# Block sums of w_out on VectorE, fifteen units of a batch's products in its own stretch, M's third quarter in other banks, a reordered end

## The chip, the core and the metric

The kernel runs on one core of a Trainium2 chip, in bf16 products with fp32 accumulation. The metric is the device time of one execution in microseconds (us). The profile calls the engines PE (TensorE), DVE (VectorE), ACT (ScalarE), POOL (GpSimd) and SP (SyncE); PEld is TensorE's weight load.

## The reference

A small two-way attention between x and a state, and then a two-layer network on both results. Every batch b has 8 heads, 512 rows of x, 32 rows of state, 64 columns:

```python
scores = scale * x @ state.T;  a  = softmax(scores);   xread = a @ state    # (8, 8, 512, 64)
scores2 = scale * state @ x.T; a2 = softmax(scores2);  sread = a2 @ x       # (8, 8, 32, 64)
y = concatenate([xread, sread], axis=2).transpose(0, 2, 1, 3).reshape(4352, 512)
h = y @ w_in                  # (4352, 2048)
g = maximum(0.01 * h, h)
out = g @ w_out               # (4352, 512), float32
```

## The kernel before

All work is in an order written out by hand, one in-order queue for each engine. A batch has a stretch of 16 steps. For batch b the kernel folds state and w_in into one matrix M (four quarters of 512 columns, `a_m` with `m_evict`), so that a step of the first layer, `ff1(a, hT, s)`, is two products of 512 columns into a PSUM bank with the tag "ph" (two banks), followed by the relu on ScalarE, which writes block s of hT. Around these products the stretch of batch b prepares the attention of batch b + 1:

- `a_scores` (PSUM tag "sc") needs `a.xT`, which `a_xt_dma` makes with a transposing DMA on SP's queue out of `a.xb`. GpSimd casts `xb` from the loaded `xl` (`cast_x`).
- `a_shift` (row maxima and subtraction), `a_max2`, `a_probs` and `a_probs2` run on VectorE; the exponentials `a_exp` and `a_exp2` on ScalarE.
- `a_a2t` transposes a2 with a DMA into `a2T`, and `a_sread` multiplies it with x (PSUM tag "big").
- `a_m` for quarter 3 of the batch itself comes in step 1, for quarters 0, 1 and 2 of the next one in steps 10, 10 and 13, in the banks "big" and "sc".

The second layer is computed in two ways. Batches 0 and 1 use `piece`: four products of 512 columns, four pieces to a block of 128 rows, and `y_store` copies the finished bank (tag "py") into a tile `ysb` (tag "ysb", three buffers) and issues its store. Batches 2 to 7 and the rows of the state (the last stretch, `hs`) use seven products in place of eight (Winograd's form of Strassen's method): `Batch` and `Fast`. The sums of blocks of hT are VectorE instructions (`Fast.sums`); the four sums of blocks of w_out, `tw`, are made once on GpSimd (`weights_sums`, in two halves). A batch has 56 units `(n, m)`, product n of block pair m, each two products of 256 columns; they run in the order of `Batch.units` in two "py" banks. When a product is complete, `done` copies the bank (`save`, ScalarE) or adds it to a copy (`join`, VectorE), and the results go from `yo0` and `yo1` to DRAM.

The loop hands units out by step: two, or three and four in turn, first those left from the batch before, then those of the batch itself:

```python
            k = OWN if b == 2 else 0
            n = 3 + s % 2 if b > 2 else 2
            left = len(before.units) if before else 0
            if left:
                before.run(min(n, left))
            if n > left:
                now.run(min(n - left, OWN - own))
                own += min(n - left, OWN - own)
```

After the loop, 16 steps of `ff1_s` (the first layer for the state's rows) alternate with units left from batch 7, and then the seven products for the state's rows with the rest.

Of the kernel before, what the change touches and what calls it, by code (L numbers as in the profile page):

```python
# [9 lines left out]
P = 128  # L10
B, H, S, D = 8, 8, 512, 64
NS = 32
# [15 lines left out]
def kernel(  # L28
# [374 lines left out]

    def weights_sums(m0, m1):
        ms = slice(m0, m1)
        for dst, u, v, op in (
            (0, B12, B11, ALU.subtract), (2, B22, B12, ALU.add),
            (1, B11, tw[2], ALU.subtract), (3, tw[1], B21, ALU.add),
        ):
            nc.gpsimd.tensor_tensor(  # L410
                out=tw[dst][:, ms], in0=u[:, ms], in1=v[:, ms], op=op
            )

    class Fast:
# [21 lines left out]

        def unit(self, bank, n, m, first):
# [7 lines left out]
            for i in range(self.sub):  # L445
                nc.tensor.matmul(  # L446
                    bank[:, i, :], lhsT=lhs[:, m, P * i:P * (i + 1)], rhs=rhs[:, m, :],
                    start=(first and m == 0 and i == 0), stop=(m == NM - 1),
                    skip_group_check=True,
                )  # L450
# [13 lines left out]
    class Batch:  # L464
        def __init__(self, b, hT):
            saved = {n: (spool, t, 1) for n, t in ((1, "sv1"), (6, "sv6"), (5, "sv1"), (7, "sv7"))}
            self.b, self.f = b, Fast(hT, 2 * P, [(spool, f"su{n}", 1) for n in range(4)], saved)
            self.units = [(n, m) for n in (1, 2, 6, 5, 7, 3, 4) for m in range(NM)]
            own = [(1, m) for m in range(6)] + [(2, m) for m in range(OWN - 6)]
            self.units = own + [u for u in self.units if u not in own]  # L470
            self.bank = {}
            self.yos = {}
# [5 lines left out]

        def out(self, r):
            nc.sync.dma_start(  # L480
                out[self.b * SROW:self.b * SROW + S, :].rearrange(
                    "(p r i) f -> p r i f", r=2, i=2)[:, r], self.yo(r)[:]
            )

# [38 lines left out]

    OWN = 10

# [251 lines left out]
    for s in range(16):  # L777
# [31 lines left out]

    before = None  # L810
    for b in range(2, B):
        hT = hpool.tile([P, 16, S], BF16, name="hT", tag="hT")
# [4 lines left out]
        if b == 2:  # L817
            std = [(i, 3) for i in range(2)] + [(i, jq) for i in range(2, NT) for jq in range(4)]
        own = 0
        for s in range(16):  # L820
            ff1(a, hT, s)
            if s == 0:
# [7 lines left out]
            elif s == 1:  # L830
# [5 lines left out]
                if b + 2 < B:  # L836
                    cast_x(b + 2, 0, 8, POO)
                if b == 2:
                    weights_sums(4, 8)
            elif s == 3:  # L840
                if before:
                    before.f.sums(2)
                if nxt is not None:
                    a_max2(nxt)
            elif s == 4:
                if b == 2:
                    load_state(1)
            elif s == 6:
                if b == 2:
                    a_sread(a1)  # L850
                if before:
                    before.f.sums(3)
            elif s == 8:
                a_sread(a)
                if b == 2:
                    state_t(1)
            if s == 11:
                for n in (0, 1):
                    now.f.sums(n, 0, 4)
            if nxt is not None:  # L860
                if s == 5:
                    a_exp(nxt)
                elif s in (6, 7):
                    a_exp2(nxt, s - 6)
                    if s == 7:
                        a_probs(nxt)
                        a_probs2(nxt)
                elif s == 10:
                    pm0 = a_m(nxt, 0, "big")
                    pm1 = a_m(nxt, 1, "sc")  # L870
                    m_evict(nxt, 0, pm0, VEC)
                    m_evict(nxt, 1, pm1, SCA)
                elif s == 13:
                    m_evict(nxt, 2, a_m(nxt, 2, "big"), SCA)
                if s == 13 and b + 2 < B:
                    a_open(att_of[b + 2], b + 2)
                    a_xt_dma(att_of[b + 2])
            if std:
                i, jq = std.pop(0)
                piece(1, h1, i, jq)  # L880
                continue
            k = OWN if b == 2 else 0
            n = 3 + s % 2 if b > 2 else 2
            left = len(before.units) if before else 0
            if left:
                before.run(min(n, left))
            if n > left:
                now.run(min(n - left, OWN - own))
                own += min(n - left, OWN - own)
        before = now  # L890
# [9 lines left out]
    for j in range(16):  # L900
        ff1_s(hs, j)
        before.run(1 + j % 2)
        if j == 5:
            before.f.sums(2)
        elif j == 8:
            before.f.sums(3)
        elif j in (9, 11):
            fs.sums((j - 9) // 2, 0, 4)
    for n in (0, 1):
        fs.sums(n, 4, 8)  # L910
    u = psum.tile([P, 1, HC], FP32, name="yu", tag="big", bufs=1)[:]
    v = psum.tile([P, 1, HC], FP32, name="yv", tag="sc", bufs=1)[:]
    ysb = [ypool.tile([P, 1, DM], FP32, name="yhs", tag="ysb") for _ in range(2)]

    def out_s(i):
        for bb in range(4):
            r0 = (4 * i + bb) * SROW + S
            nc.sync.dma_start(out[r0:r0 + NS, :], ysb[i][NS * bb:NS * (bb + 1), 0, :])

    for n in (1, 2, 6, 5, 7, 3, 4):  # L920
        bank = v if n in (2, 5, 3) else u
        for m in range(NM):
            fs.unit(bank, n, m, first=n in (1, 2, 5, 4))
        if n in (1, 6, 5, 7):
            fs.save(n, bank)
        if n == 1:
            fs.sums(2)
        elif n == 2:
            fs.join(ysb[0][:, :, :HC], bank, 1)
            fs.sums(3)  # L930
        elif n == 7:
# [6 lines left out]
        elif n == 4:  # L938
            fs.join(ysb[1][:, :, :HC], bank, 7)
            out_s(1)  # L940
        if n != 4:
            before.run(min(4, len(before.units)))
    before.run(len(before.units))

# [29 lines left out]
```

## Time and profile before

| | us |
|---|---|
| median of 3 runs | 223.9 (223.79 to 224.22) |
| the profiled execution | 223.65 |
| its span, first to last instruction | 221.9 |
| TensorE busy | 202.4 |
| VectorE busy | 151.0 |
| ScalarE busy | 142.2 |
| GpSimd busy | 48.9 |

The span is what the trace shows; the profiled execution's own time lies 1.75 us above it. TensorE's products are pipelined, so its busy time is not a count of useful cycles; gaps between the starts of its instructions say more.

### The profile page before, as it was taken

The numbers are of one execution on the slowest core, as the hardware profiler recorded it, in microseconds if no ns is written. First come the engines' busy times: TensorE is split into PE (matmuls) and PEld (weight loads), VectorE is DVE, ScalarE is ACT, GpSimd is POOL, SyncE is SP. The second block draws the span as 40 slices with busy tenths as digits, with TensorE's granted clock in tenths as the row PEclk, the third lists the DMA queues.
The fourth block names the chain that finished last, engine by engine and source line by source line (L and its number), as shares of the span: only waits on it lengthen the run. The fifth ranks groups of instructions, "written<-read, shape, count | busy, mean of one in ns | idle before, by whom it ended". The sixth has DMA issues, their size and how long they took to land.

```text
span 221.9 us, 4381 instructions
## 1 busy us (share of the span) xinstructions
PE 202.4 (91%) x1804; PEld 127.3 (57%) x1804; DVE 151.0 (68%) x205; ACT 142.2 (64%) x266; POOL 48.9 (22%) x53
## 2 busy tenths in 40 slices
PE   7999999856999778999999999999999999999980
PEld 2543434322345335666666666665666677788870
DVE  1778597089978958997799689967995613360340
ACT  3468575809869736796679677966796766556210
POOL 8830002098009910320015003200020002000210
PEclk9999999999999969999999999999999999999996
DMA  6999994991187059104990595058003300300025
GB/s 205 210 207 294 203 258 92 262 244 33 27 230 219 3 126 251 26 3 133 246 144 4 144 266 112 3 124 211 1 3 145 92 3 35 154 3 0 3 109 175
DMA packets 38020, 27.74 MB, mean 125 GB/s; under 512 B 24304, under 2 KB 34672, under 8 KB 38000
## 3 DMA queue, kind: packets, MB, share of 16 engines
q1 hardware_dynamic: 33072, 21.04, 38.2%
q0 software_dynamic: 4784, 6.29, 14.0%
q8 instruction: 14, 0.23, 0.4%
q10 hardware_dynamic: 144, 0.13, 0.2%
q14 instruction: 6, 0.05, 0.1%
HBM read 17.30 MB, written 8.91 MB: 118 GB/s over the span
## 4 chain that ended last, share of the span: by engine, by line
PE 44%; DVE 25%; DMA 17%; POOL 5%; issue 5%; SPq 1%; POOLq 0%; DVEq 0%
PE yq L446 19%; PE ph L347 8%; DMA xT<-xb 7%; DMA w_in_bf<-in_moe_w_in_dram 5%; PE pyw L375 3%; PE ph L358 3%; DMA out_dram<-ysb 3%; DVE mrowb L223 3%; DVE mrow L215 3%; DMA xl<-in_x_dram 3%; DVE su L435 3%; PE py L375 2%; DVE M L340 2%; POOL tw_xf L410 2%; DVE aT L247 2%
## 5 line engine op out<-in xcount | busy, mean ns | idle before, releaser
L352 ACT ACTIVATE hT<-ph 128x512 bf16<-128x512 f32 x112 | 66.3, 600 | 33.2 <-PE ph L347 32.5
L347 PE MATMUL ph<-aT,M 128*128 128x512 bf16 x224 | 66.2, 381 | 2.6 <-ACT hT L352 2.6
L446 PEld LDWEIGHTS <-su 128*128 128x128 bf16 x416 | 40.0, 98 | 16.5 <-issue 4.8
L446 PEld LDWEIGHTS <-hT 128*128 128x128 bf16 x288 | 27.6, 99 | 13.4 <-issue 4.2
L446 PE MATMUL yq<-tw_xf,su 128*128 128x256 bf16 x192 | 27.6, 272 | 2.0 <-DVE yo L458 2.0
L347 PEld LDWEIGHTS <-M 128*128 128x128 bf16 x224 | 21.8, 98 | 11.9 <-issue 4.4
L446 PE MATMUL yq<-w_out_bf,hT 128*128 128x256 bf16 x192 | 27.3, 278 | 0.0
L375 PE MATMUL py<-w_out_bf,hT 128*128 128x512 bf16 x96 | 24.2, 379 | 2.3 <-DVE ysb L384 2.3
L435 DVE TENSOR_TENSOR su<-hT 128x1024 bf16<-128x1024 bf16 (+1 forms) x18 | 16.6, 924 | 12.1 <-ACT hT L352 12.1
L514 POOL TENSOR_TENSOR yo<-sv,sv 128x512 f32<-128x512 f32 x6 | 8.0, 1330 | 75.7 <-ACT sv L455 53.1
L105 POOL CAST xb<-xl 128x2048 bf16<-128x2048 f32 (+1 forms) x6 | 10.7, 1776 | 63.2 <-DMA xl<-in_x_dram 63.2
L458 DVE TENSOR_TENSOR yo<-yq,sv 128x512 f32<-128x512 f32 x18 | 12.3, 686 | 16.6 <-PE yq L446 16.6
L375 PEld LDWEIGHTS <-hT 128*128 128x128 bf16 x128 | 11.9, 98 | 16.8 <-issue 3.7
L340 ACT CAST M<-pm 128x1024 bf16<-128x1024 f32 x18 | 18.2, 1011 | 5.0 <-PE pm L326 4.9
L455 ACT COPY sv<-yq 128x512 f32<-128x512 f32 x24 | 14.0, 585 | 3.3 <-PE yq L446 3.2
L446 PE MATMUL yq<-tw_x,hT 128*128 128x256 bf16 x96 | 13.5, 273 | 0.0
L446 PE MATMUL yq<-w_out_bf,su 128*128 128x256 bf16 x96 | 13.5, 273 | 0.0
L446 PE MATMUL yq<-tw_x,su 128*128 128x256 bf16 x96 | 13.4, 273 | 0.0
L340 DVE CAST M<-pm 128x1024 bf16<-128x1024 f32 x9 | 11.0, 1218 | 1.7 <-PE pm L326 1.7
L215 DVE TRANSPOSE_TENSOR_REDUCE mrow<-sc 128x32 f32<-128x1024 f32 x7 | 8.7, 1248 | 4.5 <-PE sc L205 4.5
L273 ACT ACTIVATE e<-sc,mcols 128x512 bf16<-128x512 f32 x16 | 11.1, 700 | 0.4 <-DVE mcols L267 0.4
L326 PE MATMUL pm<-w_in_bf,st_t 64*32 64x512 bf16 x192 | 8.9, 391 | 2.7 <-DVE M L340 2.7
(124 smaller groups left out, 270.1 us busy)
## 6 DMA issues: line engine op xcount, KB each, us to landing
out_dram<-yo SPq DMA_DIRECT2D x12, 512.0 KB, 2.9
xl<-in_x_dram SPq DMA_DIRECT2D x5, 1024.0 KB, 6.6
w_in_bf<-in_moe_w_in_dram POOLq DMA_DIRECT2D x4, 512.0 KB, 9.3
w_out_bf<-in_moe_w_out_dram POOLq DMA_DIRECT2D x4, 512.0 KB, 16.7
out_dram<-ysb SPq DMA_DIRECT2D x8, 256.0 KB, 5.1
xf<-in_x_dram SPq DMA_DIRECT2D x2, 512.0 KB, 5.1
x<-in_x_dram POOLq DMA_DIRECT2D x2, 512.0 KB, 13.7
xl<-in_x_dram POOLq DMA_DIRECT2D x1, 1024.0 KB, 18.5
```

Of the source, the lines that this page charges most:

```text
L105: copy(xs[b][:, :, h0:h1].rearrange("p t h d -> p h t d"), xl[b][:, h0:h1].rearrange("p h (t d) -> p h t d", t=NT),)
L215: nc.vector.tensor_reduce(out=m1[:], in_=flat.rearrange("p (c j) -> p c j", j=NS), axis=AX.X, op=ALU.max, apply_transpose=True,)
L273: nc.scalar.activation(out=a.e2[:, g], in_=a.sc[:, g, :], func=AF.Exp, bias=a.m2s[:, g:g + 1], scale=SCALE, accum_out=a.r2[:, g:g + 1],)
L326: nc.tensor.matmul(at[v][NS * r:NS * (r + 1)], lhsT=st_of(a, g, k), rhs=w_in_bf[D * g:D * (g + 1), k, DM * c:DM * (c + 1)], start=True, st ...
L340: copy(a.M[:, :, cols], pm[:])
L347: nc.tensor.matmul(ph[:], lhsT=a.M[:, g, P * j:P * (j + 1)], rhs=a.aT[:, g, :], start=(g == 0), stop=(g == 1),)
L352: nc.scalar.activation(out=hT[:, j, :], in_=ph[:], func=AF.Prelu, alpha=0.01)
L375: nc.tensor.matmul(y.py, lhsT=hT[:, j, P * i:P * (i + 1)], rhs=w_out_bf[:, j, :], start=(j == 0), stop=(j == 15),)
L435: (eng or nc.vector).tensor_tensor(out=S[n][:, ms], in0=u[:, ms], in1=v[:, ms], op=op)
L446: nc.tensor.matmul(bank[:, i, :], lhsT=lhs[:, m, P * i:P * (i + 1)], rhs=rhs[:, m, :], start=(first and m == 0 and i == 0), stop=(m == NM ...
L455: copy(t[:], bank)
L458: nc.vector.tensor_tensor(out=dst, in0=bank, in1=self.sv[n][:], op=ALU.add)
```

## The change

- `y_store` gives batch 0's blocks 2 and 3 the tags `yo0` and `yo1` (one buffer each), which the batches from 2 on use for their results. The other six blocks share the three buffers of "ysb".
- The sums of w_out's blocks become four VectorE instructions over all eight pairs, two in step 3 and two in step 8 of batch 2. `weights_open` only allocates, and moves ahead of the loop.
- A batch runs 15 of its 56 units in its own stretch in place of 10: six of product 1, six of product 2, and then (1, 6), (2, 6), (1, 7). The number of units per step is in two lists, `PACE` and, for batch 2, `PACE2`. In step 11 the units come ahead of `ff1`.
- The first three quarters of M for the next batch are all multiplied in step 10, behind its units: quarter 0 in "big", 1 in "sc", 2 in the two "ph" banks. VectorE and ScalarE copy one half each of quarter 2; ScalarE then copies quarters 0 and 1.
- `a_xt_dma` for batch b + 2 moves from step 13 to step 11, `a_exp2` from steps 6 and 7 to 7 and 8, `a_probs2` from step 7 to 11, the block sums of hT from step 11 to 12 (three of them), and those for the batch before to steps 2 and 3.
- At the end the units left are spread otherwise, half of the state's stores go to GpSimd's queue, and the last product of batch 7 is computed in two halves of rows, the second in another bank. Each half is joined and stored by itself; the right half of `yo1` is stored ahead of them.

```diff
@@ y_store
-        ysb = ypool.tile([P, DM], FP32, name="ysb", tag="ysb")
+        tag, bufs = (f"yo{i - 2}", 1) if (b, i) in ((0, 2), (0, 3)) else ("ysb", 3)
+        ysb = ypool.tile([P, DM], FP32, name="ysb", tag=tag, bufs=bufs)
@@ the sums of w_out
-    def weights_sums(m0, m1):
-        ms = slice(m0, m1)
-        for dst, u, v, op in (
...
-            nc.gpsimd.tensor_tensor(
-                out=tw[dst][:, ms], in0=u[:, ms], in1=v[:, ms], op=op
-            )
+    def weights_sum(dst):
+        u, v, op = (
+            (B12, B11, ALU.subtract), (B11, tw[2], ALU.subtract),
+            (B22, B12, ALU.add), (tw[1], B21, ALU.add),
+        )[dst]
+        with nc.allow_low_precision(reason="operands of a product"):
+            nc.vector.tensor_tensor(out=tw[dst][:], in0=u[:], in1=v[:], op=op)
@@ Batch
-            own = [(1, m) for m in range(6)] + [(2, m) for m in range(OWN - 6)]
+            own = [(n, m) for n in (1, 2) for m in range(6)] + [(1, 6), (2, 6), (1, 7)]
...
-    OWN = 10
+    OWN = 15
+    PACE = (1, 4, 4, 4, 3, 4, 4, 3, 4, 4, 4, 4, 3, 4, 3, 3)
+    PACE2 = (0,) * 10 + (3, 3, 2, 2, 2, 3)
@@ batch 1's stretch, step 8
             a_sread(a0)
-            weights_open()
-            weights_sums(0, 4)
@@ the loop over batches 2 to 7
+        def fill(s):
+            n = (PACE2 if b == 2 else PACE)[s]
+            left = min(n, len(before.units)) if before else 0
+            if left:
+                before.run(left)
+            if n > left:
+                now.run(n - left)
+
         for s in range(16):
+            if s == 11:
+                fill(s)
             ff1(a, hT, s)
...
                     cast_x(b + 2, 0, 8, POO)
-                if b == 2:
-                    weights_sums(4, 8)
+                if before:
+                    before.f.sums(2, 4, 8)
             elif s == 3:
                 if before:
-                    before.f.sums(2)
+                    before.f.sums(3)
                 if nxt is not None:
                     a_max2(nxt)
+                if b == 2:
+                    weights_sum(0)
+                    weights_sum(2)
...
             elif s == 8:
                 a_sread(a)
                 if b == 2:
                     state_t(1)
-            if s == 11:
-                for n in (0, 1):
+                    weights_sum(1)
+                    weights_sum(3)
+            elif s == 11 and b + 2 < B:
+                a_open(att_of[b + 2], b + 2)
+                a_xt_dma(att_of[b + 2])
+            elif s == 12:
+                for n in range(3):
                     now.f.sums(n, 0, 4)
             if nxt is not None:
                 if s == 5:
                     a_exp(nxt)
-                elif s in (6, 7):
-                    a_exp2(nxt, s - 6)
+                elif s in (7, 8):
+                    a_exp2(nxt, s - 7)
                     if s == 7:
                         a_probs(nxt)
-                        a_probs2(nxt)
-                elif s == 10:
-                    pm0 = a_m(nxt, 0, "big")
-                    pm1 = a_m(nxt, 1, "sc")
-                    m_evict(nxt, 0, pm0, VEC)
-                    m_evict(nxt, 1, pm1, SCA)
-                elif s == 13:
-                    m_evict(nxt, 2, a_m(nxt, 2, "big"), SCA)
-                if s == 13 and b + 2 < B:
-                    a_open(att_of[b + 2], b + 2)
-                    a_xt_dma(att_of[b + 2])
+                elif s == 11:
+                    a_probs2(nxt)
             if std:
                 i, jq = std.pop(0)
                 piece(1, h1, i, jq)
...
+            elif s != 11:
+                fill(s)
+            if s == 10 and nxt is not None:
+                pm0 = a_m(nxt, 0, "big")
+                pm1 = a_m(nxt, 1, "sc")
+                pm2 = a_m(nxt, 2, "ph")
+                for g, copy in enumerate((VEC, SCA)):
+                    copy(nxt.M[:, g, 2 * DM:3 * DM], pm2[g][:])
+                m_evict(nxt, 0, pm0, SCA)
+                m_evict(nxt, 1, pm1, SCA)
@@ the end
-        before.run(1 + j % 2)
+        before.run(1)
...
-            nc.sync.dma_start(out[r0:r0 + NS, :], ysb[i][NS * bb:NS * (bb + 1), 0, :])
+            (nc.gpsimd, nc.sync)[i].dma_start(out[r0:r0 + NS, :], ysb[i][NS * bb:NS * (bb + 1), 0, :])
...
-    for n in (1, 2, 6, 5, 7, 3, 4):
+    before.run(2)
+    for n, more in ((1, 2), (2, 2), (6, 1), (5, 1), (7, 1), (3, 0), (4, 0)):
...
-    before.run(len(before.units))
+        before.run(more)
+    before.run(8)
+    before.out(1, slice(HC, DM))
+    for i in range(2):
+        bank = before.bank[7] if i == 0 else psum.tile([P, 2, HC], FP32, name="yz", tag="ph")[:]
+        for m in range(NM):
+            before.f.unit(bank, 4, m, first=True, of=i)
+        nc.vector.tensor_tensor(
+            out=before.yo(1)[:, i, :HC], in0=bank[:, i, :], in1=before.f.sv[7][:, i, :], op=ALU.add
+        )
+        before.out(1, slice(0, HC), i)
```

## Rows read from the trace of the kernel before

**Rows 1.** The page's first part: busy us (share of the span) and instructions.

```profile
PE 202.4 (91%) x1804; PEld 127.3 (57%) x1804; DVE 151.0 (68%) x205; ACT 142.2 (64%) x266; POOL 48.9 (22%) x53
```

**Rows 2.** Waits of PE: us in total, times, longest.

```profile
PE pm L326 <- DVE M L340: 2.7, 1, 2.7
PE ph L347 <- ACT hT L352: 2.6, 2, 2.1
PE py L375 <- DVE ysb L384: 2.3, 1, 2.3
PE yq L446 <- DVE yo L458: 2.0, 4, 0.5
PE sc L205 <- DMA xT<-xb: 1.5, 3, 0.8
```

**Rows 3.** Timeline of PE in batch 1's stretch: start, duration, line, operation.

```profile
40.80 0.41 PE L205 MATMUL sc<-xT,st_t 64*32 64x512 bf16 x8
...
42.66 1.05 PE L347 MATMUL ph<-aT,M 128*128 128x512 bf16 x4
...
47.33 0.63 PE L299 MATMUL psr<-a2T,xb 128*128 128x64 bf16 x16
...
55.71 0.63 PE L326 MATMUL pm<-w_in_bf,st_t 64*32 64x512 bf16 x16
```

**Rows 4.** Timeline of DVE in the same stretch, the idle time before in brackets.

```profile
45.29 0.69 DVE L384 COPY ysb<-py 128x512 f32<-128x512 f32 x1 [6.05 <-DMA out_dram<-ysb]
```

**Rows 5.** Timeline of SP, and DMA issues of 39.8 to 40.0 (us to landing).

```profile
39.83 2.18 SPq L291 DMA_TRANSPOSE a2T<-a  x1
...
a2T<-a SPq DMA_TRANSPOSE x1, 7.0
```

**Rows 6.** Timelines of DVE and POOL in batch 2's stretch.

```profile
73.72 4.29 DVE L284 TENSOR_SCALAR a<-e,qc 128x512 bf16<-128x512 bf16 x2
...
73.54 2.13 POOL L410 TENSOR_TENSOR tw_xf<-w_out_bf,tw_x 128x1024 bf16<-128x1024 bf16 x1
```

**Rows 7.** Windows: us, busy (instructions) of PE, PEld, DVE, ACT, POOL, clock, DMA.

```profile
79.00:80.00 1.00, 0.81 (x10) 0.31 (x10) 0.97 (x3) 0.12 (x1) 0.00 (x0) 0.50 0.29 60
...
81.00:82.00 1.00, 1.00 (x5) 0.59 (x4) 0.00 (x0) 0.32 (x1) 0.00 (x0) 0.53 0.98 242
```

**Rows 8.** Groups by form: busy us, mean ns of one, idle before and releaser.

```profile
L435 DVE TENSOR_TENSOR su<-hT,su 128x2048 bf16<-128x2048 bf16 x6 | 7.3, 1217 | 0.0
...
L338 DVE CAST M<-pm 128x512 bf16<-128x512 f32 x2 | 1.3, 680 | 0.0
...
L340 ACT CAST M<-pm 128x1024 bf16<-128x1024 f32 x18 | 18.2, 1011 | 5.0 <-PE pm L326 4.9
...
L352 ACT ACTIVATE hT<-ph 128x512 bf16<-128x512 f32 x112 | 66.3, 600 | 33.2 <-PE ph L347 32.5
```

**Rows 9.** Timeline of DVE: a block sum of hT beside a GpSimd cast.

```profile
89.79 2.32 DVE L435 TENSOR_TENSOR su<-hT 128x2048 bf16<-128x2048 bf16 x1
```

**Rows 10.** The chain of waits: start, us, what.

```profile
113.62 0.87 PE yq L446 x8
```

**Rows 11.** Timeline of PE in batch 4's stretch, around the join of product 2.

```profile
111.29 0.59 PE L347 MATMUL ph<-aT,M 128*128 128x512 bf16 x2
112.37 0.81 PE L446 MATMUL yq<-tw_xf,su 128*128 128x256 bf16 x6 [0.49 <-DVE yo L458]
```

**Rows 12.** DMA issues of 102 to 103: us to landing.

```profile
xT<-xb SPq DMA_TRANSPOSE x1, 5.0
```

**Rows 13.** Timeline of DVE at the end.

```profile
215.83 0.42 DVE L458 TENSOR_TENSOR yhs<-yu,sv 128x256 f32<-128x256 f32 x1 [0.19 <-PE yu L446]
```

**Rows 14.** Timeline of SP at the end.

```profile
217.30 2.12 SPq L918 DMA_DIRECT2D out_dram<-yhs  x4
```

**Rows 15.** DMA from 212 to 222: rate in 40 slices, issues (us to landing).

```profile
GB/s 0 0 0 131 393 426 410 410 328 0 0 0 0 0 0 180 82 221 58 205 90 188 156 377 410 410 442 336 221 246 271 99 205 0 0 0 0 0 0 0
...
out_dram<-yhs SPq DMA_DIRECT2D x8, 64.0 KB, 1.7
```

More of the change, by code (lines that the diff above doesn't have):

```diff
@@ L435, in sums, with unit @@
                 (eng or nc.vector).tensor_tensor(out=S[n][:, ms], in0=u[:, ms], in1=v[:, ms], op=op)
-        def unit(self, bank, n, m, first):
+        def unit(self, bank, n, m, first, of=None):
             A, S = self.A, self.S
@@ L444, in unit @@
                 rhs = tw[{4: 3, 5: 0, 6: 1, 7: 2}[n]]
-            for i in range(self.sub):
+            for i in range(self.sub) if of is None else (of,):
                 nc.tensor.matmul(
                     bank[:, i, :], lhsT=lhs[:, m, P * i:P * (i + 1)], rhs=rhs[:, m, :],
-                    start=(first and m == 0 and i == 0), stop=(m == NM - 1),
+                    start=(first and m == 0 and (i == 0 or of is not None)), stop=(m == NM - 1),
                     skip_group_check=True,
@@ L468, in __init__ @@
             self.units = [(n, m) for n in (1, 2, 6, 5, 7, 3, 4) for m in range(NM)]
-            own = [(1, m) for m in range(6)] + [(2, m) for m in range(OWN - 6)]
+            own = [(n, m) for n in (1, 2) for m in range(6)] + [(1, 6), (2, 6), (1, 7)]
+            assert len(own) == OWN
             self.units = own + [u for u in self.units if u not in own]
@@ L477, in yo, with out @@
             return self.yos[r]
[L479 to L483, printed above, removed]
+        def out(self, r, cols=slice(0, DM), i=None):
+            rows = out[self.b * SROW:self.b * SROW + S, :].rearrange("(p r i) f -> p r i f", r=2, i=2)
+            ts = slice(0, 2) if i is None else slice(i, i + 1)
+            nc.sync.dma_start(rows[:, r, ts, cols], self.yo(r)[:, ts, cols])
         def open(self, n):
@@ L810 @@
     before = None
+    weights_open()
     for b in range(2, B):
@@ L850 @@
                     a_sread(a1)
-                if before:
-                    before.f.sums(3)
             elif s == 8:
@@ L880 @@
                 piece(1, h1, i, jq)
[L881 to L889, printed above, removed]
+            elif s != 11:
[8 more added lines that the diff above has]
+                m_evict(nxt, 1, pm1, SCA)
         before = now
@@ L901 @@
         ff1_s(hs, j)
-        before.run(1 + j % 2)
-        if j == 5:
-            before.f.sums(2)
-        elif j == 8:
+        before.run(1)
+        if j == 1:
+            before.f.sums(2, 4, 8)
+        elif j == 4:
             before.f.sums(3)
-        elif j in (9, 11):
-            fs.sums((j - 9) // 2, 0, 4)
-    for n in (0, 1):
+        elif j in (9, 10, 11):
+            fs.sums(j - 9, 0, 4)
+    for n in range(3):
         fs.sums(n, 4, 8)
+    fs.sums(3)
     u = psum.tile([P, 1, HC], FP32, name="yu", tag="big", bufs=1)[:]
     v = psum.tile([P, 1, HC], FP32, name="yv", tag="sc", bufs=1)[:]
-    ysb = [ypool.tile([P, 1, DM], FP32, name="yhs", tag="ysb") for _ in range(2)]
+    ysb = [ypool.tile([P, 1, DM], FP32, name="yhs", tag="ysb", bufs=3) for _ in range(2)]
     def out_s(i):
@@ L925 @@
             fs.save(n, bank)
-        if n == 1:
-            fs.sums(2)
-        elif n == 2:
+        if n == 2:
             fs.join(ysb[0][:, :, :HC], bank, 1)
-            fs.sums(3)
         elif n == 7:
@@ L940 @@
             out_s(1)
-        if n != 4:
-            before.run(min(4, len(before.units)))
-    before.run(len(before.units))
+        before.run(more)
[9 more added lines that the diff above has]
+        before.out(1, slice(0, HC), i)
 _INS = ['x', 'state', 'moe_w_in', 'moe_w_out']
```

4 lines of the change are left out of this document (removed).

## The prediction

> **What bounds the kernel now.** I read the page's first part, the waits, the timelines of TensorE and of the engines it waits for, and the windows for the clock. TensorE is busy for 202.4 of 221.9 us [rows 1], so time is won where its queue stands still. From about 37 us on there are five such places [rows 2]: 2.7 us for a VectorE cast of M, 2.6 us for ScalarE's relu, 2.3 us for a VectorE copy into ysb, four short waits for the yo join, and three for the transposed x. Behind the ysb copy stands a DMA: VectorE itself waits 6.05 us, to 45.29, for an older ysb buffer to be stored [rows 4]. For the rest I count queue starts on TensorE. Eight products of 256 columns, four units, take 0.87 us [rows 10], so a unit takes 0.22 us and a step's two products of 512 columns 0.43 us. "Step" is the loop index of a stretch; T is the moment at which the three quarters of M in step 10 have been issued.
>
> **Batch 1's stretch: -3.5 us.** Batch 0's last two stores take tags of their own, so the fourth ysb no longer waits for the first one's DMA. The copy of step 3 then runs when its product is ready, ahead of the scores of 40.80 [rows 3], and the maxima for batch 2 start behind those at 41.3 instead of behind the copy at 45.29 + 0.69 = 45.98 [rows 4]. The 2.3 us wait goes, and step 7's piece follows the products that start at 42.66 [rows 3]: 42.66 + 0.87 = 43.5; piece and product 8 bring TensorE to a_sread(a0) at 44.8. That is late next: it reads a2T, whose transposing DMA is issued at 39.83 and lands 7.0 us later, at 46.8 [rows 5]. Before, a_sread came at 47.33 and did not feel it. So TensorE stands about 2.0 us at a new place and starts at 46.9. From there no wait is left, because ScalarE's exponential, which stalled the relus, has its input near 45.0 (41.3 and three instructions of some 1.2): 0.47 for a_sread, 0.43 for product 9, four times 0.87 for piece, two products, piece, two products, 0.87 for the last piece and 0.1 put the two quarters of M at 52.2, against 55.71 [rows 3]. Bounds: -2.9 if the batch 0 store that is now issued earlier delays a2T by 0.6; -4.9, the 2.3 and 2.6 of rows 2, if a2T lands earlier.
>
> **Block sums from GpSimd to VectorE: -2.7 and -1.4 us.** Two scalings that VectorE runs beside the GpSimd sums take 4.29 us together, 73.72 to 78.0 [rows 6], and the M cast behind them makes TensorE wait 2.7 us [rows 2]. The clock is then granted at half, the 1.2 GHz level, in three windows from 79 to 82 us, with 0.81 and twice 1.00 us of busy time [rows 7], of which half is lost: 1.4. Without the hole I expect no fall; if the clock falls all the same, the 1.4 stays. The sums become four VectorE instructions of 128x2048, at 1.217 us as the nearest form [rows 8], 4.9 us in all. What hides them is VectorE's slack in batch 2: counting 1.2 us for a whole pass, the shift of the next batch runs from 56.8 to 60.5, the column maxima to 61.9, two sums to 64.4, the probabilities (three passes) to 68.2, two sums to 70.7, while T falls at 71.2. The cover is 0.5 us. If it is gone, the VectorE half of M's third quarter is late, and with it product 11.
>
> A VectorE sum that overlapped a GpSimd cast took 2.32 us [rows 9], against 1.217, so I allow 1 us of lateness there (bounds 0 and 2). The Trainium skill (GPSIMD Engine Reference, Key points) says that GpSimd shares its SBUF interfaces with VectorE and contends with instructions that have two SBUF inputs. The trace agrees (2.32 us); by the rule all four sums stay exposed to the casts, which this kernel keeps on GpSimd, and the time would be up to 2 us above my sum.
>
> **M's quarters in step 10: +1.2 in batch 2, +2.9 in batches 3 to 6.** The third quarter leaves step 13 and goes into both ph banks, between products 10 and 11. VectorE empties one half (0.680), ScalarE the other (0.6 as for a relu of the same shape), then the two whole quarters (1.011 each), and only then relu 11 (0.600) [rows 8]. ScalarE starts 0.1 behind T; the durations add up to 3.2, neighbours overlap somewhat, so relu 11 ends at about T + 3.1 (bounds 2.8 and 3.3). Product 13 needs the bank that relu 11 frees. Until then TensorE has four units, product 11, product 12 and three units: 0.87 + 0.43 + 0.43 + 0.65 = 2.4. It waits 0.73 us, four times: 2.9. Product 11 itself waits for VectorE's half at T + 0.87, just covered by the four units. In batch 2 step 11 has three units and step 12 two: 0.22 at product 11 (0.7 if VectorE is late) and the rest at product 13, together 1.2. If ScalarE kept up, both terms would be 0; the upper end is 0.95 for each of four batches and 2.5 for batch 2.
>
> **Fifteen units: -2.6 us.** Products 1 and 2 are nearly done in the batch's own stretch, so the join of product 2 follows one unit of the next step 0, ahead of the maxima in VectorE's queue. Before it stood behind them: TensorE's products from 111.29 end at 111.72 and the next unit starts at 112.37 [rows 11], 0.65 us, in four batches. The units add up to the same number, so moving them costs nothing. The copy of product 1 goes to ScalarE behind relu 15, covered by 1.7 us of TensorE work before product 6 reads that bank. Cost of the opposite: 0, if the wait came back at product 6.
>
> **The transpose of x two steps earlier: -1.5 us** [rows 2]. On SP's queue it now stands behind the store of yo1, issued at about T + 1.6 when the last join of the batch before is done; the transpose starts at T + 1.95 and lands 5.0 us later [rows 12] at T + 6.95. The scores that need it come at about T + 7.6. Load and a2T behind it move up too, and a_sread in step 8 is 9 us away. Without the hole at product 13 the margin would be nothing.
>
> **The end: -1.9 us.** TensorE's last product ends near 215.7, and the last join starts at 215.83 [rows 13]. Four stores of 0.53 us each are then issued from 217.30 on SP [rows 14], and they land in 1.7 [rows 15], some 5.2 us after TensorE's end. Now four of the state's stores go to POOL's queue, the other four come 3 us earlier, and the last store (128 KB) is issued about 0.6 after the end. Ahead of it on the wires are 0.9 MB; the peak rate here is 410 to 440 GB/s [rows 15], so the 1.05 MB need 2.6 us, begin to flow near 0.1 after the end and are confirmed at about 3.4. Bounds: -0.5 (the queue does not drain faster) and -2.7 (only the last store counts). The Trainium skill (DMA: Bandwidth & Descriptors, Anatomy of one DMA) puts a fixed 2.0 us on each DMA whatever its size, which speaks against cutting a store in pieces. By it the last store would take an estimated 2.3 us where the row has 1.7 for 64 KB, and the end term would be about -2.3.
>
> **Sum.** -3.5 - 2.7 - 1.4 + 1.2 + 2.9 - 2.6 - 1.5 - 1.9 = -9.5 us. Against the profiled execution's own 223.65 us that is 214.15; the median of the runs shown lies 0.25 above, so I say **214.2 us**.
>
> **Rivals.** (a) ScalarE keeps up in step 10. For it: ScalarE is idle just ahead of T. Against: those durations in one in-order queue [rows 8]. It takes away 2.9 and 0.7: 210.6 us. (b) VectorE is late at step 10, since the casts on GpSimd slow its sums. Then product 11 waits in five batches. For it: 2.32 us [rows 9]; against: from step 0 of a batch I count two half sums and the join (2.1), the shift (3.7), a half and a whole sum (1.8, and 0.9 more beside a cast), the column maxima (1.4), the probabilities (3.9) and a join (0.7), so VectorE is free near 13.5 to 14.4, and T falls at 15.3. With 0.5 us a batch: 216.7. The rule of shared interfaces in the Trainium skill (GPSIMD Engine Reference, Key points) would be at work here. (c) The same place decides the sign: the lateness is paid five times, so from 1.9 us a batch on (9.5 / 5) the kernel is slower than before; at 2.5 us it is 226.7. Against it: VectorE would have to lose another 3 us or more in every batch. (d) The end is not shortened, because the same megabyte is stored: 215.6.
>
> **Chances.** Forecast 0.59, (a) 0.16, (b) 0.12, (c) 0.03, (d) 0.10. Range: (a) and (b) lie inside 210 to 217.3, and the bounds of the single terms reach hardly beyond, since they fall on both sides. A change under 0.2% is about what a measurement of this kernel cannot tell from none. Faster 0.96, within it 0.01, slower 0.03.
>
> **What would show it.** In the new profile: no ysb wait, a TensorE wait of about 2 us at L299 for a2T near 45 us; no POOL sums and a clock at 1.00 from 70 to 90; a wait of about 0.7 us for hT at each step 13; none for yo or xT; less than 4.5 us between TensorE's end and the span's. I am wrong if VectorE's half quarter holds product 11 for long, if the relu wait is missing, or if the earlier stores delay a2T by microseconds.

## The result, and the profile after

The changed kernel takes a median of 214.82 us (214.07 to 215.89, 4 runs) where the kernel before took 224.06 (223.79 to 224.76, 4 runs): a ratio of 0.9587, 95% interval 0.9531 to 0.9642. Its profiled execution took 215.48 us, 8.2 less than that of before. Of four kernels below (relu11_first, xt_step13, relu11_xt10, own10) the profiled execution is over 1.5% longer than the fastest of the same kernel; the ratios leave such executions out, the medians do not, and no ratio rests on these profiles.

The page's first part of the kernel after, which answers to [rows 1]: GpSimd has 15.7 us less to do.

```profile
PE 199.5 (93%) x1804; PEld 126.6 (59%) x1804; DVE 146.6 (69%) x217; ACT 144.4 (68%) x271; POOL 33.2 (16%) x49
```

The waits of TensorE after, from 37 us on, which answer to [rows 2] (us in total, times, longest):

```profile
PE psr L299 <- DMA a2T<-a: 3.2, 1, 3.2
PE ph L347 <- ACT hT L352: 2.8, 5, 0.6
...
PE sc L205 <- DMA xT<-xb: 0.5, 1, 0.5
...
PE ph L347 <- DVE M L895: 0.2, 1, 0.2
```

The waits for ysb, for the yo join and for the M cast at L326 are gone. Two places are new: one for a2T at L299, and a relu at step 13 of five batches. The timeline of TensorE after shows both: batch 1's stretch (the first four lines), step 10 of batch 3, and the end.

```profile
41.14 0.41 PE L205 MATMUL sc<-xT,st_t 64*32 64x512 bf16 x8 [0.52 <-DMA xT<-xb]
...
44.75 0.59 PE L347 MATMUL ph<-aT,M 128*128 128x512 bf16 x2
48.57 0.64 PE L299 MATMUL psr<-a2T,xb 128*128 128x64 bf16 x16 [3.23 <-DMA a2T<-a]
...
53.89 0.62 PE L326 MATMUL pm<-w_in_bf,st_t 64*32 64x512 bf16 x16
...
93.90 0.61 PE L445 MATMUL yq<-tw_x,hT 128*128 128x256 bf16 x4
...
95.65 0.82 PE L445 MATMUL yq<-w_out_bf,hT 128*128 128x256 bf16 x6
97.03 0.59 PE L347 MATMUL ph<-aT,M 128*128 128x512 bf16 x2 [0.57 <-ACT hT L352]
...
207.49 1.04 PE L445 MATMUL yz<-tw_x,hT 128*128 128x256 bf16 x8
```

The idle time in brackets counts from the modelled end of the matmuls ahead. Counted by queue starts, as the prediction counts, the hole at product 13 is larger: six products (three units of 0.22 us) from 95.65 hand over at 96.30, and TensorE goes on at 97.03, so it loses 0.73 us.

The chain of waits after shows what fills both places (start, us, what):

```profile
36.47 4.26 DMA xT<-xb
40.73 7.80 DMA a2T<-a
...
48.57 0.64 PE psr L299 x16
...
94.06 0.58 ACT M L895
94.65 1.83 ACT M L340 x2
96.48 0.51 ACT hT L352
...
97.03 0.59 PE ph L347 x2
```

In batch 1's stretch the chain lies on SP's queue and the transfers; in step 10 it is ScalarE: half a quarter, two quarters, and only then relu 11, which ends at 96.99, with T (here 93.90) 3.1 us earlier.

VectorE's timeline after: the ysb copy that no longer waits for a DMA, the first and the last of the four block sums, and the half quarter behind them.

```profile
40.23 0.69 DVE L385 COPY ysb<-py 128x512 f32<-128x512 f32 x1 [1.24 <-PE py L375]
...
65.10 1.21 DVE L411 TENSOR_TENSOR tw_xf<-w_out_bf 128x2048 bf16<-128x2048 bf16 x1
...
72.39 1.23 DVE L411 TENSOR_TENSOR tw_x<-tw_xf,w_out_bf 128x2048 bf16<-128x2048 bf16 x1
73.53 0.68 DVE L895 CAST M<-pm 128x512 bf16<-128x512 f32 x1
```

The window of the kernel after that answers to [rows 7] (us, busy of PE, PEld, DVE, ACT, POOL, clock, DMA): the granted clock stays at its upper level.

```profile
78.00:82.00 4.00, 4.00 (x42) 2.49 (x41) 3.14 (x4) 3.39 (x6) 0.00 (x0) 1.00 1.07 261
```

The end after, from 203 us to the span's end at 213.7: the rate in 40 slices and the DMA issues (KB each, us to landing), which answer to [rows 15].

```profile
GB/s 0 0 0 0 0 0 0 0 0 0 0 0 8 207 276 138 276 92 353 222 283 245 276 414 398 413 348 356 360 364 352 306 169 27 0 0 0 0 0 0
...
out_dram<-yo SPq DMA_DIRECT2D x1, 512.0 KB, 3.4
...
out_dram<-yo SPq DMA_DIRECT2D x1, 256.0 KB, 3.8
out_dram<-yo SPq DMA_DIRECT2D x2, 128.0 KB, 3.0
```

TensorE ends at 207.49 + 1.04 = 208.53, the span 5.2 us later. Before it was 6.2.

### The profile page after: what moved, and what is told of

The parts are those of the page before. It is cut to its first block, busy times and chain, and to the rows that moved or that the text cites. A ratio compares the mean times of both kernels' runs of the same rounds, so it can differ in the third digit from the quotient of the medians.

```text
span 213.7 us, 4395 instructions
## 1 busy us (share of the span) xinstructions
PE 199.5 (93%) x1804; PEld 126.6 (59%) x1804; DVE 146.6 (69%) x217; ACT 144.4 (68%) x271; POOL 33.2 (16%) x49
## 4 chain that ended last, share of the span: by engine, by line
PE 68%; DMA 18%; ACT 7%; SPq 2%; POOL 2%; issue 1%; DVE 1%; POOLq 0%
PE yq L445 31%; PE ph L347 19%; DMA x<-in_x_dram 7%; PE py L375 6%; ACT M L340 4%; DMA a2T<-a 4%; PE ph L358 3%; DMA stf<-in_state_dram 3%; PE pm L326 3%; DMA xf<-in_x_dram 3%; DMA xT<-xb 2%; PE psr L299 2%; PE yu L445 2%; ACT M L895 1%; SPq L169 1%; PE yv L445 1%
## 5 line engine op out<-in xcount | busy, mean ns | idle before, releaser
L352 ACT ACTIVATE hT<-ph 128x512 bf16<-128x512 f32 x112 | 65.6, 602 | 25.2 <-PE ph L347 24.6
L347 PE MATMUL ph<-aT,M 128*128 128x512 bf16 x224 | 64.8, 379 | 3.0 <-ACT hT L352 2.8
L434 DVE TENSOR_TENSOR su<-hT 128x1024 bf16<-128x1024 bf16 x24 | 19.1, 794 | 14.2 <-ACT hT L352 14.2
L457 DVE TENSOR_TENSOR yo<-yq,sv 128x512 f32<-128x512 f32 x17 | 11.6, 685 | 11.6 <-PE yq L445 11.6
L445 PE MATMUL yq<-tw_x,su 128*128 128x256 bf16 x96 | 13.9, 273 | 0.0
L445 PE MATMUL yq<-tw_x,hT 128*128 128x256 bf16 x88 | 12.1, 273 | 0.0
L265 DVE TENSOR_REDUCE mcol<-sc 128x2 f32<-128x1024 f32 x8 | 9.7, 1214 | 0.0
L358 PE MATMUL ph<-sr_t,w_in_bf 128*128 128x256 bf16 x64 | 9.6, 273 | 0.0
```

The costliest lines, as they stand in the source:

```text
L265: nc.vector.tensor_reduce(out=m2[:], in_=a.sc[:], axis=AX.X, op=ALU.max, negate=True)
L347: nc.tensor.matmul(ph[:], lhsT=a.M[:, g, P * j:P * (j + 1)], rhs=a.aT[:, g, :], start=(g == 0), stop=(g == 1),)
L352: nc.scalar.activation(out=hT[:, j, :], in_=ph[:], func=AF.Prelu, alpha=0.01)
L358: nc.tensor.matmul(ph[:, :n], lhsT=w_in_bf[:, k, P * j:P * (j + 1)], rhs=sr_t[:, k, :], start=(k == 0), stop=(k == NK - 1),)
L434: (eng or nc.vector).tensor_tensor(out=S[n][:, ms], in0=u[:, ms], in1=v[:, ms], op=op)
L445: nc.tensor.matmul(bank[:, i, :], lhsT=lhs[:, m, P * i:P * (i + 1)], rhs=rhs[:, m, :], start=(first and m == 0 and (i == 0 or of is not No ...
```

## The experiments

**The same kernel again** (after_again).

> The changed kernel as it stands, as the reference for the three runs beside it. Expected: the ratio of the first measurement, 0.9587, within its interval (0.953 to 0.964), so 214 to 216 us. Its own runs were 1.8 us apart (214.07 to 215.89) where those of the kernel before were 1.0 apart. Theory: the spread comes from a_sread(a0) in batch 1's stretch, which now waits 3.2 us for a transposing DMA whose landing hangs on early loads. Rival: the spread is elsewhere (the end, the clock).

It took 214.13 us (213.82 to 216.73, 6 runs), ratio 0.9557 (0.9509 to 0.9605). The runs lie in two groups, four from 213.8 to 214.3 and two above 216, and the runs of the result above do the same (214.07 and 214.16; 215.48 and 215.89). This profile, of an execution of 213.9 us, is of the lower group. Its waits of TensorE:

```profile
PE psr L299 <- DMA a2T<-a: 1.8, 1, 1.8
```

and its SP timeline; the kernel after has 24.63 and 40.73 us for the same two starts:

```profile
23.71 3.63 SPq L169 DMA_DIRECT2D stf<-in_state_dram  x8
...
39.94 2.64 SPq L291 DMA_TRANSPOSE a2T<-a  x1
```

The wait for a2T is 1.4 us shorter here, and M's two quarters of batch 1's stretch start at 52.35 in place of 53.89. The 1.5 us between these two profiles arise there and nowhere else: TensorE's end differs by the same 1.5. They begin at 23 us, where VectorE's cast of x waits longer for its load (1.41 us in the profile after, 0.71 here); there the loads of the state are issued 0.9 later, and so is everything behind them on SP's queue. I call this the late start. For a difference between two profiles this is shown; that every execution of the upper group has the late start is not. The clock can have a part, as the profile of xt_step13 below shows: the two upper executions here have a mean granted clock of 0.987 and 0.986, the lower four 0.993 to 1.000.

**a2T's transpose ahead of the 1 MB load of x** (a2t_first), the kernel after with one move, which also takes the transpose ahead of two stores:

```diff
-    load_x(3, nc.sync)
     open_xb(3)
     a_probs(a1)
+    a_probs2(a0)
+    a_a2t(a0)
+    load_x(3, nc.sync)
 ...
     cast_x(3, 0, 8, POO)
-    a_probs2(a0)
-    a_a2t(a0)
```

> a_probs2(a0) and the transposing DMA of a2T come right behind a_probs(a1), ahead of the 1 MB load of x for batch 3 and of two stores on SP's queue; all else as in the changed kernel. Theory (a2T lands late because it queues behind the load): it lands near 42.5 instead of 48.5 us, the 3.2 us wait at a_sread(a0) vanishes, ScalarE's chain gives back 0.6 to 0.9, and the time falls by 2 to 2.6 us to 212.2 to 212.8; the spread of the runs shrinks. Rival (the delayed load of x takes the place of a2T: the scores of batch 3 wait for xT near 55 us): the gain is under 1 us.

It took 212.61 us (212.34 to 213.48), ratio 0.9459 (0.9429 to 0.9489); the kernel after had 0.9557 on the same chip, so 2.2 us less. SP's timeline and the DMA issue (us to landing):

```profile
37.75 1.76 SPq L291 DMA_TRANSPOSE a2T<-a  x1
39.60 0.55 SPq L99 DMA_DIRECT2D xl<-in_x_dram  x1
```

```profile
a2T<-a SPq DMA_TRANSPOSE x1, 3.7
```

Ahead of the load and the two stores the same transpose lands in 3.7 us instead of 7.8, and TensorE has no wait at L299 left. The place and the price of the new wait are shown; load and stores were not moved apart. Five runs lie within 1.1 us and no longer in two groups. This profile has the early start (the state's loads at 23.69), so that the transpose would cover a late one is argued from the times and not seen in a trace.

**Relu 11 ahead of quarter 1** (relu11_first). ScalarE copies quarter 1 of M behind relu 11 instead of ahead of it:

```diff
             ff1(a, hT, s)
+            if s == 11 and nxt is not None:
+                m_evict(nxt, 1, pm1, SCA)
 ...
                 m_evict(nxt, 0, pm0, SCA)
-                m_evict(nxt, 1, pm1, SCA)
```

> ScalarE copies quarter 1 of M only behind relu 11, instead of ahead of it; all else as in the changed kernel. Theory (ScalarE's queue holds product 13 in five batches, 0.53 to 0.57 us each): relu 11 ends 0.9 us earlier, those waits vanish, and the time falls by 2.0 to 2.8 us against the changed kernel, to 212.0 to 212.8. Rival (ScalarE has no slack anyway, the wait moves to product 14 or 15 or to the scores that need the bank of quarter 1): a change of less than 0.6 us, with a wait for hT or for the sc bank in another step.

It took 215.15 us (212.49 to 217.85), ratio 0.9512 (0.9461 to 0.9564): beside 0.9557 that is 1.0 us less, with intervals that overlap. TensorE's waits:

```profile
PE sc L205 <- DMA xT<-xb: 4.5, 3, 2.6
...
PE ph L347 <- ACT hT L352: 0.3, 1, 0.3
```

The relu wait went, as the first theory has it, and the scores then wait for the transposed x, as the rival has it. In batch 4 T is 113.50; the transpose is issued at 115.97 and lands 6.0 us later, at T + 8.5, while TensorE wants it at T + 7.0. With the hole at product 13 it wants it at T + 7.8. In batch 5 the same wait is 2.59 us, and behind it TensorE runs at the 1.2 GHz level from 147 to 150 us. What this profile could not price, the next but one of the experiments did.

**The transpose of x back in step 13** (xt_step13), the kernel after with `s == 11` put back to `s == 13` for `a_open` and `a_xt_dma`.

> The changed kernel with the transposing DMA of x back in step 13 of the loop. Theory: SP's queue holds the same instructions in the same order, since no other SP instruction stands between steps 11 and 13, so nothing changes (within 0.3 us); the transposes come earlier because the joins and the stores ahead of them on the queue do. Rival (the step itself counts, two steps are 2.4 us, and the margin of the scores is 0.7): scores wait about 1.7 us in four batches, +5 to +7 us.

It took 213.88 us (213.59 to 217.69), ratio 0.9553 (0.9518 to 0.9589), against 0.9557 and 0.9587 for the kernel after: no change. The order of the instructions on SP's queue is the same either way, and an in-order queue issues the transpose when the store of yo1 ahead of it has been issued. So it is not the step in which the line stands that removed the xT wait.

The profile, of the one execution of 217.69 us, shows besides what a late start can cost. The state's loads are issued at 24.89, and the a2T wait is as long as in the profile after; but behind it the clock is granted at half, the 1.2 GHz level:

```profile
48.72 0.97 PE L299 MATMUL psr<-a2T,xb 128*128 128x64 bf16 x16 [3.22 <-DMA a2T<-a]
...
55.69 0.63 PE L326 MATMUL pm<-w_in_bf,st_t 64*32 64x512 bf16 x16
```

```profile
49.00:52.00 3.00, 3.00 (x19) 1.36 (x17) 2.86 (x5) 1.79 (x5) 0.00 (x0) 0.50 1.16 227
```

From a_sread to M's quarters it takes 6.97 us, where both profiles of the kernel after take 5.32, so the level costs 1.65, and M's quarters are back at the 55.71 of before. The profiles of relu11_xt10 and own10 show the same fall behind the same wait (3.13 and 3.40 us), that of end_actq does not (3.33).

**Both, with the transpose ahead of yo1's store** (relu11_xt10): relu11_first with `s == 10` for `a_open` and `a_xt_dma`, which on SP's queue comes before that store.

> As the run with relu 11 ahead of quarter 1's copy, and besides the transposing DMA of x is issued in step 10, so that on SP's queue it stands ahead of the store of yo1 instead of behind it. In the run with relu 11 first the waits for hT were gone, but the scores waited 1.4 and 2.6 us for xT. Theory (xT hangs on the store of yo1 ahead of it, whose join comes only in step 11): xT lands about 2 us earlier, no wait is left there, and the time is 2.0 to 2.8 us below the changed kernel, 211.4 to 212.4. Rival (the transposes are slowed by the traffic beside them, not by their place on the queue): waits for xT of 1 us or more stay, the time is above 213.5.

It took 213.55 us (210.37 to 214.52), ratio 0.941 (0.9349 to 0.9471): 2.3 us below relu11_first and 3.3 below the kernel after (0.9557), by ratios of two chips; the intervals of the first pair still touch. The median lies above the 213.5 that I had named for the rival, but the waits decide against it: from batch 2 on no xT wait is left. This profile has the late start and the fall of the clock behind its a2T wait of 3.1 us. Of the other waits of TensorE there remain:

```profile
PE sc L205 <- DMA xT<-xb: 0.5, 1, 0.5
PE ph L347 <- ACT hT L352: 0.4, 1, 0.4
```

So the hole at product 13 is worth its 3 us only if the transpose comes earlier too.

**All three edits** (three_edits): relu11_xt10 and a2t_first together.

> The run before this one with a2T ahead of the load of x in batch 0's end as well. Theory (the two gains lie in different stretches and add up): 2.0 to 2.8 below the run with a2T first (212.6), so 209.8 to 210.6, and no run above 212. Rival (some other queue sets the pace once both are gone): above 211.5.

It took **209.22 us** (208.56 to 209.97), ratio 0.9313 (0.928 to 0.9346), the fastest kernel of the study: 5.5 us below the kernel after by the ratios (0.9557). The waits of TensorE that are left from 37 us on, and the window from 90 to 156 us, where the kernel after had TensorE busy for 64.28 of 66 us:

```profile
PE ph L347 <- ACT hT L352: 0.4, 1, 0.4
PE ph L347 <- DVE M L897: 0.3, 1, 0.3
```

```profile
90.00:156.00 66.00, 65.47 (x624) 46.12 (x619) 55.80 (x82) 53.20 (x97) 7.74 (x5) 1.00 0.52 122
```

**ysb tags alone** (only_ysb), the kernel before with this part of the change:

```diff
-        ysb = ypool.tile([P, DM], FP32, name="ysb", tag="ysb")
+        tag, bufs = (f"yo{i - 2}", 1) if (b, i) in ((0, 2), (0, 3)) else ("ysb", 3)
+        ysb = ypool.tile([P, DM], FP32, name="ysb", tag=tag, bufs=bufs)
```

> The kernel before with one part of the change alone: batch 0's blocks 2 and 3 in the tags yo0 and yo1. Theory: the wait for the ysb copy (2.3 us) and ScalarE's stalls behind it (2.6) go, a wait of 2 to 3 us for a2T at a_sread(a0) comes, net -1.5 to -2.5 us, so 221.5 to 222.5. Rival: the GpSimd sums, whose second half waits for the load of x in batch 2, hold the M cast at the same moment as before, so that the 2.7 us wait there grows by what was won: -0.5 to 0.

It took 222.35 us (220.83 to 223.92, 10 runs), ratio 0.9923 (0.9884 to 0.9961), so -1.7 us; the profiled execution, with a late start (24.68), is only 0.8 below that of before. Its waits, and one pair of scalings on VectorE:

```profile
PE pm L326 <- DVE M L340: 3.8, 2, 2.7
PE psr L299 <- DMA a2T<-a: 3.6, 1, 3.6
```

```profile
53.61 4.24 DVE L284 TENSOR_SCALAR a<-e,qc 128x512 bf16<-128x512 bf16 x2
```

The ysb wait is replaced by the a2T wait, and M's quarters start at 54.33 where before has 55.71 [rows 3]. Part of these 1.4 us is given back later: the scalings above now lie beside GpSimd's sums (48.65 to 57.70), where before they began at 57.42, behind them (54.68), and took 0.62 a pair; a second M cast comes late, by 1.1 us, and the xT waits add up to 2.8 us instead of 1.5.

**Block sums on VectorE alone** (only_sums), the kernel before with `weights_sum` at steps 3 and 8 of batch 2, as in the change.

> The kernel before with another part alone: the four block sums of w_out on VectorE in steps 3 and 8 of batch 2. Theory: the 2.7 us wait for the M cast goes, the clock stays at full (1.4), nothing takes their place: -3.5 to -4.5 us, so 219.5 to 220.5. Rival: a sum on VectorE is paid where a sum on GpSimd was (4.9 us of VectorE work ahead of the M cast in step 10): -2 us or less, with a wait for the cast left in step 13.

It took 220.29 us (219.81 to 221.14), ratio 0.9849 (0.9812 to 0.9886), so -3.4 us, where the two terms of the prediction add up to -4.1. The waits of TensorE that are of interest, and VectorE's timeline:

```profile
PE py L375 <- DVE ysb L384: 2.6, 1, 2.6
...
PE pm L326 <- DVE M L340: 1.5, 1, 1.5
```

```profile
65.37 1.23 DVE L410 TENSOR_TENSOR tw_xf<-w_out_bf 128x2048 bf16<-128x2048 bf16 x1
66.52 2.91 DVE L410 TENSOR_TENSOR tw_x<-w_out_bf 128x2048 bf16<-128x2048 bf16 x1
```

The M cast still waits 1.5 of its 2.7 us, because the sums of step 8 stand ahead of it and one sum took 2.91 us while GpSimd cast xb (65.53 to 68.35). So the sums alone shorten the wait; that it is gone altogether in the kernel after takes the other parts too. In this profile TensorE gains 2.5 us between M's quarters (55.64) and its end (213.17): 1.1 of the hole, and the 1.4 of the clock, which stays at its upper level there. It falls instead at 46 to 49 us, beside the ysb wait.

**The old end** (old_end), the kernel after with the tail of the kernel before: all eight stores of the state's rows last, from SP, the units handed out as before, and no split of the last product.

```diff
-    before.run(2)
-    for n, more in ((1, 2), (2, 2), (6, 1), (5, 1), (7, 1), (3, 0), (4, 0)):
+    for n in (1, 2, 6, 5, 7, 3, 4):
 ...
-        before.run(more)
-    before.run(8)
-    before.out(1, slice(HC, DM))
 ...
+        if n != 4:
+            before.run(min(4, len(before.units)))
+    before.run(len(before.units))
```

> The changed kernel with the end of the kernel before (order of units and products, one queue for the stores, the last product in one piece). Theory: the new end won 6.1 - 5.1 = 1.0 us, so 0.8 to 1.2 us above the changed kernel, 215.6 to 216.0. Rival (the same megabyte is stored, the end is worth nothing): within 0.3 us of it.

It took 216.48 us (214.54 to 218.13), ratio 0.9699 (0.9647 to 0.975). The profiles are the better comparison, since they share the early start: old_end has a span of 212.8 with TensorE's end at 206.67, a tail of 6.1; after_again 212.1 and 207.04, a tail of 5.1. So the new end is worth 1.0 us of tail. TensorE ends 0.4 later in after_again, but 0.3 of that stands already at M's quarters in batch 1's stretch (52.35 against 52.04), so the end hardly costs TensorE anything. The ratios would make it more, 2.5 to 3.2 us; of the three executions compared one is near 214.5 and two near 216.5, the spacing of the two groups above, so I take the profiles' value, and a larger one is not excluded.

**The last stores from ScalarE's queue** (end_actq), the kernel after with `eng=nc.scalar` for the last three stores of `out`.

> The last three stores (right half of yo1, then the two left halves) are issued from ScalarE's queue instead of SP's; all else as in the changed kernel. Theory (the end, 5.1 us behind TensorE's last product instead of the 4.2 forecast, is held by SP, which issues four stores between 207.5 and 210.5): the last store is issued about 1 us earlier and the time falls by 0.6 to 1.0 us. Rival (the wires are full: 1 MB at 350 to 410 GB/s): the change is within 0.3 us.

It took 214.47 us (214.08 to 216.3), ratio 0.9556 (0.9517 to 0.9596), against 0.9557: no change. The DMA issues of its end (KB each, us to landing):

```profile
out_dram<-yo ACTq DMA_DIRECT2D x1, 256.0 KB, 3.1
...
out_dram<-yo ACTq DMA_DIRECT2D x2, 128.0 KB, 3.9
```

So the issue is not the limit. The last store is out 0.5 us sooner after TensorE's end (ScalarE's queue has issued at 210.29, TensorE ends at 208.87; 210.48 and 208.53 in the profile after), and the tail is still 5.4 us. The Trainium skill (DMA: Bandwidth & Descriptors, Issuing engines are not separate DMA queues) says that DMAs from all issuers run on the same 16 engines and interleave, so that a second issuer only saves issue time. The trace agrees: the 128 KB stores land in 3.9 us where they took 3.0, the 512 KB store in 4.3 where it took 3.4, and only the 256 KB one sooner (3.1, where it took 3.8). That the DMA engines themselves are the limit fits with this and is not shown further.

**Ten units instead of fifteen** (own10), the kernel after with the old list of a batch's own units. Five more units of batch 7 are then left for the end, which runs them there:

```diff
-            own = [(n, m) for n in (1, 2) for m in range(6)] + [(1, 6), (2, 6), (1, 7)]
+            own = [(1, m) for m in range(6)] + [(2, m) for m in range(4)]
 ...
-    OWN = 15
+    OWN = 10
 ...
-    PACE2 = (0,) * 10 + (3, 3, 2, 2, 2, 3)
+    PACE2 = (0,) * 10 + (2, 2, 2, 2, 2, 0)
 ...
-    before.run(8)
+    before.run(len(before.units) - 8)
```

> The changed kernel with ten units of a batch in its own stretch instead of fifteen (six of product 1, four of product 2), the units per step as in the change; five more units are left for the end. Theory (the fifteen matter because they bring the join of product 2 ahead of the maxima in VectorE's queue): the join stands behind the maxima again, product 5 waits for it about 1.2 us in four batches, and the scores of the next batch wait for xT, since the last join and its store come a step later: 4 to 6 us above the changed kernel, 218 to 220. Rival (only the number of units per step counts): within 1 us of it.

It took 221.35 us (218.15 to 222.65), ratio 0.9761 (0.9696 to 0.9827), 3.9 to 4.6 us above the kernel after by its two ratios, which rest on two executions here. The yo waits are back, in four batches:

```profile
PE yq L445 <- DVE yo L457: 4.4, 4, 2.1
```

In batch 3 the join starts at 86.28 behind maxima that VectorE runs from 81.50 on. In the profile after it runs at 80.15, ahead of them. So the fifteen units are what takes the join out from behind the maxima. The waits for xT that I had also expected did not show (0.5 us, once).

## Why the prediction was right, step by step

The profiled execution took 215.48 us where the sum says 214.15, and the medians 214.8 and 214.1 lie on both sides of 214.2. Most mechanisms came as forecast, but that the sum comes so close is in part luck: it counted 0.9 us too much at the end and some 1.2 too little in the middle. By stretches, from TensorE's starts in both traces (stretch: from the second pair of products, 38.55 before, to M's quarters, 55.71 [rows 3]; middle: from there to TensorE's end, 215.72 before; tail: to the span's end):

| | forecast | profile after | after_again |
|---|---|---|---|
| ahead of the stretch | 0 | -0.25 | -0.2 |
| batch 1's stretch | -3.5 | -1.6 | -3.15 |
| the middle | -4.1 | -5.35 | -5.3 |
| the tail | -1.9 | -1.0 | -1.1 |
| sum | -9.5 | -8.2 | -9.75 |

**Batch 1's stretch: mechanism right, size left to chance.** The copy, the new wait and its place are as forecast: a_sread at 46.9 was the forecast, 47.0 is after_again's, and 48.57 that of the profile after. The step that was mis-sized is "lands 7.0 us later, at 46.8": the row came from an execution in which the state's loads had started early, at 23.82; in the profile after they start at 24.63, a2T is issued 0.9 later and takes 7.8. I had bounded the landing by a store that moves, and not by the start of the queue, which varies from run to run. The sum also puts at nothing that the new hole can bring the clock down as the old one did: in three of the six profiles with a late start it does, for 1.5 to 1.7 us, and in xt_step13's nothing is left of the 3.5. The 0.5 us for xT at 41.14 was not in the sum.

**Block sums and the clock.** The hole of 2.7 us [rows 2] is gone, the four sums take 1.21 to 1.23 us each, and the half quarter starts 0.84 us behind T, where I had allowed 1; it costs 0.35 by queue starts. The bank that waits for it is that of product 12 (74.27), and product 11 takes the one that ScalarE empties; the prediction had VectorE's half at product 11. Of the rule weighed there (the Trainium skill, GPSIMD Engine Reference, Key points) the runs show both sides: in the kernel after GpSimd's cast ends at 65.17, just as the first sum starts, and no sum is slowed; in only_sums one that runs beside the cast took 2.91.

The 1.4 us of the clock did come back, since the window stays at 1.00. But that the hole caused the fall is not shown: only_ysb has the same hole at the same place, 2.72 us until 79.06, and its granted clock stayed at 1.00 behind it:

```profile
79.00:80.00 1.00, 0.94 (x13) 0.61 (x13) 0.97 (x3) 0.47 (x1) 0.00 (x0) 1.00 0.61 125
80.00:81.00 1.00, 1.00 (x9) 0.66 (x7) 0.33 (x1) 1.00 (x2) 0.00 (x0) 1.00 0.91 258
```

So the 1.4 belongs to the execution that I summed against, and the only_sums run, 0.7 short of -4.1, is no proof of it either: in its profile the level falls elsewhere. What decides whether it falls stays open.

**M's quarters.** Relu 11 ends at T + 3.1 as worked out, and product 13 waits 0.73 us by queue starts in four batches, exactly the term of 2.9; batch 2 pays 0.35 and 0.69, 1.04 of 1.2. Rival (a), that ScalarE keeps up, and rivals (b) and (c), that VectorE is late in every batch, are refuted by the same waits: VectorE's half holds TensorE once, for 0.2 us.

**Yo join and xT.** The four joins are gone (2.6), and own10 shows that it is the list of units that did it. The xT wait is gone as well (1.5 by idle time, some 2.0 by queue starts), but its heading, "two steps earlier", named the wrong part of the diff: xt_step13 changes nothing. What the sum really rested on, the place behind the store of yo1 with a margin that the hole at product 13 provides, held: relu11_first took the hole away and the scores waited. Only the margin was smaller than the forecast 0.65 us: in batches 4 and 5 of the profile after the transpose takes 5.8 and 5.4 us in place of 5.0 and lands at 123.57 and 145.55, just ahead of the scores of 123.62 and 145.57.

With these by queue starts the middle gives -2.8 - 1.4 - 2.6 - 2.0 + 1.0 + 2.9 = -4.9 of the -5.35; the other 0.45 stands in no wait.

**The end.** "The peak rate here is 410 to 440 GB/s" was the step too many. The volume was right: the slices from 208.6 to 212.1 sum to 1.08 MB. But it flowed in 13 slices of 0.27 us, 3.5 us and not 2.6, at 348 to 414 GB/s in the eight best of them and slower ahead of these and behind. These 0.9 us are the whole miss. The 2.0 us of the rule on small DMAs decided nothing: 128 KB took 3.0 us to land, behind other stores, and before, 64 KB took 1.7 [rows 15]. The Trainium skill (DMA: Bandwidth & Descriptors, Anatomy of one DMA) gives that figure for DMAs that GpSimd issues, and these came from SP. The tail of less than 4.5 us that I named as a sign did not come; the gain, 1.0, lies between rival (d)'s bound of 0.5 and the forecast.

## What to carry to other kernels

When a wait goes, look at what the next consumer needs and how long its transfer stands behind others on the same in-order queue: a transpose of 3.7 us took 7.8 behind a 1 MB load and two stores, and moving it was worth 2.2 us. Two waits can cover one another, as the relu hole covered the transpose of x, so an edit that looks worthless alone can pay 3 us with its partner. A duration that ends in a DMA should be read from several executions, and an edit credited by the queue order that it changes, not by the line that moves.

## What the runs showed of the hardware that was not expected

- One load of x lands about 0.9 us later in some executions, and SP's in-order queue carries that on. In the profiles in which the new a2T wait stands, it is 1.7 to 1.9 us where the state's loads are issued at 23.7, and 3.1 to 3.6 where they are issued at 24.5 to 24.9. That is 1.5 us at TensorE's end in two profiles of the kernel after.
- Holes on TensorE and the clock: of ten waits of 2.6 to 3.6 us in these profiles, six came with the 1.2 GHz level (2.67 in before, 2.64 in only_sums, 2.59 in relu11_first, 3.22 in xt_step13, 3.13 in relu11_xt10, 3.40 in own10) and four did not (3.23 in the profile after, 3.33 in end_actq, 2.72 and 3.63 in only_ysb). The length of the wait does not tell which.
- VectorE beside GpSimd: a pair of scalings took 4.24 us in place of 0.62, and one sum of 128x2048 took 2.91 in place of 1.22, while the sum just ahead of it, whose span also lies over the cast's, took 1.23. GpSimd's cast beside them took 2.82, against 1.89 in the profile after.
